# A spectral block's forward stage as a written plan of single steps, with all of xn on VectorE

## The chip, the cores and the metric

The kernel runs on one core of a Trainium2 chip. The metric is the time of one execution on the device in microseconds, the median of three runs. In the profile PE is TensorE's matmuls and PEld its weight loads, DVE is VectorE, ACT is ScalarE, POOL is GpSimd, SP is the engine that issues most DMAs.

## The reference, cut to what matters

```python
x = A_x                                                     # (1, 2048, 640) bf16
sa, ca, ga, sb, cb, gb = silu(c) @ w_mod, in six rows of 640
h = layernorm(x) * (1 + ca) + sa
x = x + ga * irfft2(rfft2(h) * (w_r + 1j * w_i))            # spectral mixing
h = layernorm(x) * (1 + cb) + sb
x = x + gb * ((silu(h @ w_gate) * (h @ w_up)) @ w_down)     # 1728 hidden columns
```

The two-dimensional Fourier transforms over 2048 x 640 are done as matmuls with tables of cosines and sines.

## The kernel before

The 2048 rows are 16 tiles of 128 rows (row = 16 p + t). Everything is emitted in the order in which it stands in the code: the schedule is manual, each engine executes its instructions in that order, and a tile framework adds the semaphore waits. A pool with `bufs=n` gives n buffers to one name; the next tile of that name waits until the oldest is free.

**Head** (lines 201 to 231 and 353 to 381). SP issues all early loads in one order: x tiles, `wm_ca`, the DFT table `Rp`, the tables `Gtab`, then the spectral weights (`Wneg`, `Wb`, `Wq`), `wm_sa`, `Ktab` and `wm_g`; none of them waits for compute. TensorE runs warm-up matmuls (`keep_warm`, `w_ps`), 44 and later 6. `mod_cols` (25 matmuls with one column) gives 1 + ca, and `Rs` is `Rp` scaled by it, four pieces on VectorE and two on ScalarE.

**Forward stage** (L277 to L426). For a tile t:

- statistics: two `bn_stats` halves and an aggregate on VectorE (`st`, `mv`; L280, L282)
- rstd: a square root on ScalarE (L251), a reciprocal on VectorE (L292); from tile 4 on for two tiles at once
- xn = (x - mean) * rstd (L297): on VectorE, and on GpSimd for tiles 7, 9, 11 and 13
- five transposes on TensorE into `t1ps` (L303), copied from PSUM to `hT`: by ScalarE (L306) for odd tiles and tile 0, by VectorE (L308) otherwise
- dfwd: six matmuls of 328 columns with `Rs` into `zps` (L319), copied to Z by ScalarE (L327), for tile 14 by VectorE
- s1: four matmuls of 328 columns with `Gtab` into `aps` (L331, L332; one buffer), copied by ScalarE into `A_sb` (L345)

Tile 15 goes in two halves (`zE`, `zO`, `apsh`). A loop over t interleaves square roots, transposes and statistics of later tiles with dfwd(t) and s1(t - 1). After t = 14 VectorE negates the spectral weights in two instructions (L425, L426). `mod_sa` (25 matmuls into `mpsB`, then `sa_col` on VectorE) ends the stage.

**Product stage** (L448 to L619). Columns are worked in 11 units, ten of them with four groups and one, the third, with a single group; the first three are transposed by TensorE (`t2`, copied to `B2`), the others by DMA transposes that SP issues when `A_sb` is full and Gtab's memory is free. A unit: `stage_a` (`xps`, copied to X by ScalarE; GpSimd then adds `shat` to one partition of X), `product` (PP, VectorE), `stage_b` (`yps`, L498; copied to Y2), `stage_c` (`eps_`, copied to Ep by ScalarE). `mod_shat` computes `shat` from `sa_col`: six matmuls into `sps`, E to SBUF on ScalarE, two `scalar_tensor_tensor` on VectorE. In the first round of the loop `m_ps` (50 matmuls) gives the gates' columns, which ScalarE copies out. After it come the inverse transforms (L677 to L722) and the feed-forward (L732 to the end).

The loop of the forward stage, in its core:

```python
for t in range(2, NT + 1):
    if t % 2 == 0 and t < NT - 2:
        ln1_sqrt(t + 2, t + 4)
    if 4 <= t < NT - 1:
        t1(t + 1)
...
    if 4 <= t < NT:
        dfwd(t)
    if t >= 4:
        s1(t - 1)
```

Of the kernel before, what the change touches and what calls it, by code (L numbers as in the profile page):

```python
# [18 lines left out]
LH = 164  # L19
# [116 lines left out]
def adaln_block_kernel(  # L136
# [46 lines left out]
    sE = const.tile([1, 2, LH], F32, name="sE")  # L183
# [87 lines left out]
    with tc.tile_pool(name="ph1", bufs=3) as ph1, \  # L271
# [5 lines left out]
        def ln1_half(t, h):  # L277
            if h == 0:
                sts[t] = ph1.tile([P, 2, 6], F32, name="st")
            nc.vector.bn_stats(sts[t][:, h, :], x_sb[:, t, 320 * h:320 * h + 320])  # L280
            if h == 1:
                nc.vector.bn_aggr(mv1[:, t, :], sts.pop(t)[:])  # L282

        def ln1_stats(t):
            ln1_half(t, 0)
            ln1_half(t, 1)
# [7 lines left out]
        def ln1_xn(t):  # L294
            xns[t] = ph1.tile([P, D], BF16, name="xn")
            eng = nc.gpsimd if t in (7, 9, 11, 13) else nc.vector
            eng.tensor_scalar(xns[t][:], x_sb[:, t, :], mv1[:, t, 0:1], rstd1[:, t:t + 1], ALU.subtract, ALU.mult)  # L297

        def t1(t):
            xn = xns.pop(t)  # L300
            t1ps = ps1.tile([P, NC5, 128], BF16, name="t1ps")
            for c5 in range(NC5):
                nc.tensor.transpose(t1ps[:, c5, :], block(xn, c5), identb[:])  # L303
            hTs[t] = ph1.tile([P, NC5, 128], BF16, name="hT")
            if t % 2 == 1 or t == 0:
                nc.scalar.copy(hTs[t][:], t1ps[:])  # L306
            else:
                nc.vector.tensor_copy(hTs[t][:], t1ps[:])  # L308

        def dfwd(t):  # L310
            hT = hTs.pop(t)
            if t == NT - 1:
                zs = [ps1.tile([P, 512], F32, name=n, tag="t1ps") for n in ("zE", "zO")]
            else:
                zps = ps1.tile([P, 2, 512], F32, name="zps")
                zs = [zps[:, 0], zps[:, 1]]
            for r in range(2):
                for i in range(3):
                    nc.tensor.matmul(zs[r][:, :L], lhsT=hT[:, 2 * r + i, :], rhs=Rs[:, 3 * r + i, :],  # L319
                                     start=(i == 0), stop=(i == 2))  # L320
            if t == NT - 1:
                Zs[t] = [ph1.tile([P, L], BF16, name=n, bufs=1) for n in ("ZE", "ZO")]
                nc.scalar.copy(Zs[t][0][:], zs[0][:, :L])
                nc.vector.tensor_copy(Zs[t][1][:], zs[1][:, :L])
            else:
                Zs[t] = ph1.tile([P, 2, 2, LH], BF16, name="Z")
                (nc.vector.tensor_copy if t == NT - 2 else nc.scalar.copy)(Zs[t][:].rearrange("p r c l -> p r (c l)"), zps[:, :, :L])  # L327
# [5 lines left out]

        def s1(t):
            Z = Zs.pop(t)
            if t == NT - 1:
                for r, eng in ((0, nc.scalar.copy), (1, nc.vector.tensor_copy)):
                    aps = ps1.tile([P, 2, 256], F32, name="apsh", tag="zps")
                    s1_into(t, [aps[:, c, :LH] for c in range(2)], Z[r][:, 0:LH], Z[r][:, LH:L])
                    eng(A_sb[:, NG * r:NG * r + NG, t].rearrange("p l c j -> p c l j"),  # L340
                        aps[:, :, :LH].rearrange("p c (l j) -> p c l j", j=4))
                return
            aps = ps1.tile([P, 2, 512], F32, name="aps", tag="aps", bufs=1)
            s1_into(t, [aps[:, c, :L] for c in range(2)], Z[:, :, 0, :], Z[:, :, 1, :])
            nc.scalar.copy(A_sb[:, :, t, :, :].rearrange("p l c j -> p c l j"),  # L345
                           aps[:, :, :L].rearrange("p c (l j) -> p c l j", j=4))

        def mod_sa():
            mpsB = ps1.tile([P, NC5], F32, name="mpsB", tag="t1ps")
            mod_cols(mpsB, wm_sa, 0, True)  # L350
            nc.vector.tensor_copy(sa_col[:], mpsB[:])
# [4 lines left out]
        keep_warm(ps1, "t1ps", 2, 44)  # L356
# [3 lines left out]
        ln1_stats(0)  # L360
        ln1_sqrt(0, 1)
        ln1_stats(1)
        ln1_sqrt(1, 2)
        ln1_recip(0, 1)
        ln1_xn(0)
        ln1_recip(1, 2)
        ln1_xn(1)
# [3 lines left out]
        t1(0)  # L371
# [6 lines left out]
        t1(1)  # L378
        keep_warm(ps1, "t1ps", 2, 6)
        ln1_stats(2)  # L380
        ln1_sqrt(2, 3)
        dfwd(0)
        dfwd(1)
        ln1_half(3, 0)
        ln1_recip(2, 3)
        ln1_xn(2)
        ln1_half(3, 1)
        ln1_sqrt(3, 4)
        t1(2)
        s1(0)  # L390
        ln1_half(4, 0)
        ln1_recip(3, 4)
        ln1_xn(3)
        ln1_half(4, 1)
        dfwd(2)
        t1(3)
        s1(1)
        ln1_stats(5)
        for t in range(2, NT + 1):
            if t % 2 == 0 and t < NT - 2:  # L400
                ln1_sqrt(t + 2, t + 4)
            if 4 <= t < NT - 1:
                t1(t + 1)
            if t == 3:
                dfwd(3)
                s1(2)
                t1(4)
            if t + 4 < NT:
                ln1_half(t + 4, 0)
            if t % 2 == 0 and t + 2 < NT:  # L410
                ln1_recip(t + 2, t + 4)
                if t + 3 in (7, 9, 11, 13):
                    ln1_xn(t + 3)
            if t + 2 < NT and t + 2 not in (7, 9, 11, 13):
                ln1_xn(t + 2)
            if t + 4 < NT:
                ln1_half(t + 4, 1)
            if 4 <= t < NT:
                dfwd(t)
            if t >= 4:  # L420
                s1(t - 1)
            if t == NT:
                mod_sa()
            if t == 14:
                nc.vector.tensor_scalar_mul(Wb[:, 0, :, 0:161], Wb[:, 2, :, 0:161], -1.0)  # L425
                nc.vector.tensor_scalar_mul(Wq[:, 2], Wq[:, 0], -1.0)  # L426
# [10 lines left out]
    with tc.tile_pool(name="ph2", bufs=2) as ph2, \  # L437
# [13 lines left out]
        def t2(u):  # L451
            n = len(units[u])
            for h in range(2):
                t2ps = ps2.tile([P, 4, 128], BF16, name="t2ps", bufs=2)
                for i, g in enumerate(units[u]):
                    nc.tensor.transpose(t2ps[:, i, :], A_sb[:, NG * h + g, :, :, :].rearrange("p t c j -> p (t c j)"), identb[:])
                B2 = ph2.tile([P, 4, 128], BF16, name="B2", bufs=4)
                if h == 0:
                    nc.scalar.copy(B2[:, :n, :], t2ps[:, :n, :])
                else:  # L460
                    nc.vector.tensor_copy(B2[:, :n, :], t2ps[:, :n, :])
                for i, g in enumerate(units[u]):
                    B2s[NG * h + g] = B2[:, i, :]
# [76 lines left out]
        def mod_shat(l0, l1):  # L540

            sps = ps2.tile([1, 2, 256], F32, name="sps", tag="eps_", bufs=2)
            n = 2 * (l1 - l0)
            for r in range(2):
                for i in range(3):
                    nc.tensor.matmul(sps[:, r, :n], lhsT=sa_col[:, 2 * r + i:2 * r + i + 1],
                                     rhs=Rp[:, 3 * r + i, :].rearrange("p (c l) -> p c l", c=2)[:, :, l0:l1],
                                     start=(i == 0), stop=(i == 2))
            E = sE[:, :, l0:l1]
            O = sps[:, 1, :n].rearrange("p (c l) -> p c l", c=2)  # L550
            nc.scalar.activation(E, sps[:, 0, :n].rearrange("p (c l) -> p c l", c=2), ACT.Copy, scale=float(S))
            for h in range(2):
                nc.vector.scalar_tensor_tensor(shat[:, h, :, l0:l1], O, float(S) if h == 0 else -float(S), E, ALU.mult, ALU.add)

        t2(0)
        mod_shat(128, LH)
        Xs[0] = stage_a(0)
        t2(1)
        for it in range(NU + 2):
            if it == 0:  # L560
                PPs[0] = [product(0, 0, Xs[0][0])]
# [4 lines left out]
            if it == 0:  # L566
                mod_shat(0, 128)
                m_ps = ps2.tile([P, 2, NC5], F32, name="m_ps", tag="eps_", bufs=2)
# [5 lines left out]
            if it < NU:  # L574
                X = Xs.pop(it)
                if it > 0:
                    PPs[it] = [product(it, 0, X[0])]
            if 0 <= it - 1 < NU:
                PP = PPs.pop(it - 1)
                Y2s[it - 1] = []  # L580
                for h in range(len(PP)):
                    yps = stage_b(it - 1, h, PP[h])
                    Y2s[it - 1].append(evict_y(it - 1, h, yps))
            if it < NU and len(X) > 1:
                PPs[it].append(product(it, 1, X[1]))
            if it == 1:
# [249 lines left out]
```

## Time and profile before

| | us |
|---|---|
| median of three runs (lowest, highest) | 284.66 (284.05, 284.86) |
| the profiled execution | 284.62 |
| its span | 282.40 |
| head, to the first matmul of dfwd(0) | 0 to 9.2 |
| forward stage, to the first matmul of `mpsB` | 9.2 to 41.3 |
| bridge, to the second unit's first `yps` | 41.3 to 51.2 |
| other units | to 77.4 |
| inverse transforms | 77.4 to 101.0 |
| feed-forward | 101.0 to 282.4 |

How to read it: times count from the start of the span. A row of a group gives line, engine, operation, output and inputs, then busy time, the mean of one in ns, and the idle time of the engine just before it with what ended it. A row of the waits gives the waiting engine, tile and line, then who released it: total, how often, the longest. The chain of waits is followed back from the last instruction to what released each step; it gives start, length and step. A wait for several things is put down to the last.

### The profile page before, as it was taken

To read this page: it belongs to the slowest core of one execution; us is meant where nothing else is said; L and a number is where in the kernel's file an instruction comes from. 1 tells how busy PE (TensorE), PEld (TensorE's weight loads), DVE (VectorE), ACT (ScalarE), POOL (GpSimd) and SP (SyncE) were. 2 spreads that over 40 slices of the span, in tenths; PEclk is the share of its full clock that TensorE was granted. 3 is DMA by queue.
4 is the path that set the end of the run, shared out by engine and by line. 5 is a ranking of instruction groups with operands and counts; after the bars stand their busy time and mean duration, and the time that the engine had idled before them with its cause. 6 is when DMAs were issued, how large, how long until landed. Compare 5 with 4: busy or idle time off the path is not lost.

```text
span 282.4 us, 5282 instructions
## 1 busy us (share of the span) xinstructions
PE 269.8 (96%) x2130; PEld 171.1 (61%) x2130; DVE 161.9 (57%) x408; ACT 114.0 (40%) x221; POOL 19.0 (7%) x34
## 2 busy tenths in 40 slices
PE   7979988999899999999999999999999999999995
PEld 7556667999687854445764445774444675444673
DVE  4897654799769847887225863323882422432322
ACT  5769875899555673223013224004223203223000
POOL 0026501322000010000000000000000000000000
PEclk9999999999999999999999999999999999999999
DMA  7979969999793401040110031011004011000011
GB/s 266 417 204 240 372 238 165 248 328 375 261 328 118 71 12 23 0 95 0 46 49 12 0 51 44 23 49 33 0 7 88 24 47 34 0 1 2 0 46 46
DMA packets 40634, 30.82 MB, mean 109 GB/s; under 512 B 29281, under 2 KB 37410, under 8 KB 40482
## 3 DMA queue, kind: packets, MB, share of 16 engines
q1 hardware_dynamic: 40608, 30.49, 36.9%
q8 instruction: 16, 0.26, 0.4%
q14 instruction: 8, 0.07, 0.1%
q10 hardware_dynamic: 2, 0.00, 0.0%
HBM read 22.88 MB, written 3.93 MB: 95 GB/s over the span
## 4 chain that ended last, share of the span: by engine, by line
PE 84%; DVE 7%; ACT 4%; POOL 2%; issue 1%; DMA 0%; ACTq 0%; POOLq 0%; DVEq 0%
PE gps L750 20%; PE ups L750 20%; PE ob L784 11%; PE oa L784 10%; PE yps L498 3%; PE zps L319 3%; POOL xn L297 2%; PE oa L699 2%; PE w_ps L267 2%; PE xps L473 2%; PE xps L474 2%; PE gu L737 2%; PE ob L699 1%; DVE x_sb L702 1%; PE t1ps L303 1%
## 5 line engine op out<-in xcount | busy, mean ns | idle before, releaser
L750 PE MATMUL gps<-h2T_all,Wg 128*128 128x512 bf16 x260 | 64.6, 379 | 0.0
L750 PE MATMUL ups<-h2T_all,Wu 128*128 128x512 bf16 x260 | 64.6, 379 | 0.0
L753 ACT ACTIVATE sg<-gps 128x512 f32<-128x512 f32 x52 | 31.1, 597 | 74.0 <-PE gps L750 72.3
L750 PEld LDWEIGHTS <-Wu 128*128 128x128 bf16 x260 | 25.4, 98 | 30.7
L750 PEld LDWEIGHTS <-Wg 128*128 128x128 bf16 x260 | 25.3, 98 | 30.5
L754 DVE TENSOR_TENSOR ATb<-ups,sg 128x512 bf16<-128x512 f32 x26 | 17.9, 690 | 32.0 <-PE ups L750 32.0
L754 DVE TENSOR_TENSOR ATa<-ups,sg 128x512 bf16<-128x512 f32 x26 | 17.9, 688 | 20.4 <-PE ups L750 17.5
L784 PEld LDWEIGHTS <-ATa 128*128 128x128 bf16 x224 | 21.9, 98 | 9.3 <-issue 0.5
L784 PEld LDWEIGHTS <-ATb 128*128 128x128 bf16 x224 | 21.9, 98 | 8.8
L740 ACT ACTIVATE sg<-gu 64x512 f32<-64x512 f32 x4 | 2.3, 587 | 46.6 <-PE gu L737 46.6
L786 DVE TENSOR_TENSOR xo<-ob,x_sb 128x320 bf16<-128x320 f32 x16 | 7.9, 491 | 22.1 <-PE ob L784 22.1
L786 DVE TENSOR_TENSOR xo<-oa,x_sb 128x320 bf16<-128x320 f32 x16 | 7.8, 490 | 18.4 <-PE oa L784 18.4
L784 PE MATMUL oa<-Wd_sb,ATa 128*128 128x320 bf16 x112 | 16.8, 299 | 0.1
L784 PE MATMUL oa<-Wd_sb,ATb 128*128 128x320 bf16 x112 | 16.5, 299 | 0.0
L784 PE MATMUL ob<-Wd_sb,ATb 128*128 128x320 bf16 x112 | 16.5, 299 | 0.0
L784 PE MATMUL ob<-Wd_sb,ATa 128*128 128x320 bf16 x112 | 16.5, 299 | 0.0
L319 PE MATMUL zps<-Rs,hT 128*128 128x328 bf16 x90 | 15.0, 303 | 0.6 <-ACT hT L306 0.4
L280 DVE BATCH_NORM_STATS2 st<-x_sb 128x6 f32<-128x320 bf16 x32 | 14.4, 472 | 0.8 <-DMA x_sb<-in_A_x_dram 0.8
L691 ACT CAST VT<-va 128x512 bf16<-128x512 f32 x16 | 9.4, 587 | 8.0 <-PE va L687 7.1
L498 PE MATMUL yps<-identb,PP 128*128 128x128 bf16 x162 | 11.7, 219 | 0.6 <-DVE PP L489 0.4
L297 POOL TENSOR_SCALAR xn<-x_sb,mv,rstd 128x640 bf16<-128x640 bf16 x4 | 10.6, 2656 | 21.3 <-PE zps L319 19.3
L476 ACT CAST X<-xps 128x512 bf16<-128x512 f32 (+1 forms) x21 | 11.3, 598 | 1.4 <-PE xps L474 1.4
(204 smaller groups left out, 415.4 us busy)
## 6 DMA issues: line engine op xcount, KB each, us to landing
out_dram<-xo SPq DMA_DIRECT2D x16, 160.0 KB, 1.8
Wg<-in_B_w_gate_dram SPq DMA_DIRECT2D x1, 2080.0 KB, 12.3
Wd_sb<-in_B_w_down_dram SPq DMA_DIRECT2D x1, 2080.0 KB, 13.1
Wu<-in_B_w_up_dram SPq DMA_DIRECT2D x1, 2080.0 KB, 8.4
x_sb<-in_A_x_dram SPq DMA_DIRECT2D x3, 640.0 KB, 9.2
wm_g<-in_w_mod_dram SPq DMA_DIRECT2D x2, 800.0 KB
Gtab<-tab_G SPq DMA_DIRECT2D x4, 384.0 KB, 7.8
Htab<-tab_H SPq DMA_DIRECT2D x1, 1536.0 KB, 7.7
```

Of the source, the lines that this page charges most:

```text
L280: nc.vector.bn_stats(sts[t][:, h, :], x_sb[:, t, 320 * h:320 * h + 320])
L297: eng.tensor_scalar(xns[t][:], x_sb[:, t, :], mv1[:, t, 0:1], rstd1[:, t:t + 1], ALU.subtract, ALU.mult)
L319: nc.tensor.matmul(zs[r][:, :L], lhsT=hT[:, 2 * r + i, :], rhs=Rs[:, 3 * r + i, :], start=(i == 0), stop=(i == 2))
L476: nc.scalar.copy(X[:, :n].rearrange("p i c k j -> p i (c k j)"), xps[:, :n, :])
L498: nc.tensor.matmul(yps[:, i, :], lhsT=PP[:, i, cp].rearrange("p a k j -> p (a k j)"), rhs=identb[:], start=(cp == 0), stop=(cp == 1))
L691: nc.scalar.copy(VTs[t][:, 0:4, :], va[:])
L699: nc.tensor.matmul(os_[odd][:], lhsT=VT[:, 2 * odd + ci if ci < 2 else 4, :], rhs=Rinv_sb[:, odd, ci, :], start=(ci == 0), stop=(ci == 2))
L750: nc.tensor.matmul(o[:], lhsT=w_[:, c5, fc * 128:(fc + 1) * 128], rhs=h2T[:, :, c5, :], start=(c5 == 0), stop=(c5 == NC5 - 1))
L753: nc.scalar.activation(sg[:], gps[:], ACT.Silu)
L754: nc.vector.tensor_tensor(AT[:, fc, :], ups[:], sg[:], ALU.mult)
L784: nc.tensor.matmul(os_[h][:], lhsT=AT[:, fc, tok], rhs=Wd_sb[:, fc, h * 320:(h + 1) * 320], start=(fc == 0), stop=(fc == NFC - 1))
L786: nc.vector.tensor_tensor(xo[:, h * 320:(h + 1) * 320], os_[h][:], x1[:, t, h * 320:(h + 1) * 320], ALU.add)
```

## The change

The forward stage's loop is replaced by a string of single steps that a small interpreter emits in that order. A step is a letter and a tile: `s` with `a` or `b` is one half of the statistics, `g` the aggregate, `q` the square root, `r` the reciprocal, `n` xn, `T` the transposes, `h` the copy to hT, `D` dfwd, `Z` its copy, `S` s1, `A` its copy, `W` a negation; `d`, `z`, `u`, `v` are second halves of tile 15. What one function emitted together (transposes and their copy, statistics and aggregate) can now stand apart, so each engine gets an order of its own.

- xn is always on VectorE. The copies hT of tiles 6, 8, 10, 11, 12, 14, 15, Z of 13 and 14, and A of 10 and 11 are on VectorE, all others on ScalarE (before: hT of even tiles from 2 on and Z of 14 on VectorE).
- xn, hT and Z have four buffers instead of three, the statistics six.
- Head: 32 warm-up matmuls instead of 44; xn(0) comes before the rest of tile 1's statistics; tile 0's transposes and hT come before `mpsA`; 8 warm-ups instead of 6 after tile 1's transposes.
- The negations are cut in four: two at the end of the plan, two after the first `t2`.
- `sa_col` is copied by ScalarE. In `mod_shat` ScalarE copies E and O together and GpSimd adds and subtracts them. The B2 copies of the one-group unit are both on ScalarE.
- Both products of unit 0 come at once; `m_ps` and its copies move from the first round of the loop to the second, behind `stage_b` of unit 0.

```diff
         def ln1_xn(t):
-            xns[t] = ph1.tile([P, D], BF16, name="xn")
-            eng = nc.gpsimd if t in (7, 9, 11, 13) else nc.vector
-            eng.tensor_scalar(xns[t][:], x_sb[:, t, :], mv1[:, t, 0:1], rstd1[:, t:t + 1], ALU.subtract, ALU.mult)
+            xns[t] = ph1.tile([P, D], BF16, name="xn", bufs=4)
+            nc.vector.tensor_scalar(xns[t][:], x_sb[:, t, :], mv1[:, t, 0:1], rstd1[:, t:t + 1], ALU.subtract, ALU.mult)
...
+        def negate(i):
+            k = 8 * (i % 2)
+            o, a = ((Wb[:, 0, k:k + 8, 0:161], Wb[:, 2, k:k + 8, 0:161]), (Wq[:, 2, k:k + 8], Wq[:, 0, k:k + 8]))[i // 2]
+            nc.vector.tensor_scalar_mul(o, a, -1.0)
...
-            nc.vector.tensor_copy(sa_col[:], mpsB[:])
+            nc.scalar.copy(sa_col[:], mpsB[:])
...
-        keep_warm(ps1, "t1ps", 2, 44)
+        keep_warm(ps1, "t1ps", 2, 32)
...
+        HT_DVE, Z_DVE, A_DVE = [6, 8, 10, 11, 12, 14, 15], [13, 14], [10, 11]
+        pairs = {0: 1, 1: 2, 2: 3, 3: 4, 4: 6, 6: 8, 8: 10, 10: 12, 12: 14, 14: 16}
+        plan = (
+            "s2a D0 h1 s2b s3a D1 Z0 s3b g2 g3 S0 q2 q3 r2 Z1 r3 n2 A0 n3 T2 s5a T3 h2 s5b S1 s4b h3 D2 g5 s4a A1 "
+            "s6a D3 Z2 g4 s7a q4 s6b S2 Z3 r4 n4 A2 n5 T4 g6 T5 s7b h4 S3 s9a h5 g7 D4 s10a q6 s9b A3 D5 r6 n7 Z4 "
+            "n6 T7 s8b Z5 T6 g9 S4 h6 h7 s8a D6 A4 s10b g8 g10 S5 q8 s11b Z6 r8 D7 n8 A5 n9 T8 s13b Z7 S6 h8 T9 "
+            "s11a A6 D8 s12a h9 g11 s14a S7 s12b q10 Z8 D9 r10 n11 A7 n10 T11 g12 Z9 s13a T10 S8 h10 h11 D10 A8 "
+            "g13 s14b q12 s15a S9 Z10 r12 D11 n12 A9 g14 n13 T12 s15b Z11 S10 h12 T13 g15 A10 q14 D12 h13 r14 n14 "
+            "S11 Z12 n15 T14 A11 T15 D13 h14 h15 S12 Z13 D14 A12 S13 Z14 d15 A13 D15 z15 S14 Z15 u15 W0 A14 S15 "
+            "v15 A15 W1"
+        )
...
+        go("s0a s0b g0 q0 s1a r0 n0 s1b g1 q1 r1 n1 T0 h0")
         mpsA = ps1.tile([P, NC5], F32, name="mpsA", tag="aps", bufs=1)
         mod_cols(mpsA, wm_ca, 0, True)
...
-        t1(1)
-        keep_warm(ps1, "t1ps", 2, 6)
...
-            if t == 14:
-                nc.vector.tensor_scalar_mul(Wb[:, 0, :, 0:161], Wb[:, 2, :, 0:161], -1.0)
-                nc.vector.tensor_scalar_mul(Wq[:, 2], Wq[:, 0], -1.0)
+        go("T1")
+        keep_warm(ps1, "t1ps", 2, 8)
+        go(plan)
+        mod_sa()
...
-                if h == 0:
+                if h == 0 or n == 1:
                     nc.scalar.copy(B2[:, :n, :], t2ps[:, :n, :])
...
-            nc.scalar.activation(E, sps[:, 0, :n].rearrange("p (c l) -> p c l", c=2), ACT.Copy, scale=float(S))
+            nc.scalar.activation(sEO[:, :, :, l0:l1], sps[:, :, :n].rearrange("p r (c l) -> p r c l", c=2), ACT.Copy, scale=float(S))
             for h in range(2):
-                nc.vector.scalar_tensor_tensor(shat[:, h, :, l0:l1], O, float(S) if h == 0 else -float(S), E, ALU.mult, ALU.add)
+                nc.gpsimd.tensor_tensor(shat[:, h, :, l0:l1], sEO[:, 0, :, l0:l1], sEO[:, 1, :, l0:l1],
+                                        ALU.add if h == 0 else ALU.subtract)
 
         t2(0)
+        negate(2)
+        negate(3)
         mod_shat(128, LH)
...
             if it == 0:
-                PPs[0] = [product(0, 0, Xs[0][0])]
+                PPs[0] = [product(0, h, X) for h, X in enumerate(Xs.pop(0))]
...
             if it == 0:
                 mod_shat(0, 128)
+            if 0 < it < NU:
+                X = Xs.pop(it)
+                PPs[it] = [product(it, 0, X[0])]
+            if 0 <= it - 1 < NU:
+                PP = PPs.pop(it - 1)
...
+            if 0 < it < NU and len(X) > 1:
+                PPs[it].append(product(it, 1, X[1]))
+            if it == 1:
                 m_ps = ps2.tile([P, 2, NC5], F32, name="m_ps", tag="eps_", bufs=2)
                 mod_cols(m_ps[:, 0], wm_g, 0)
                 mod_cols(m_ps[:, 1], wm_g, 1)
```

## The prediction

> **What bounds the kernel now.** The profiled execution took 284.62 us: a span of 282.40 and 2.22 around it; the median of the three runs is 284.66, so sums made on this execution are moved by +0.04. I read the page's first two parts, then the busy time by stretch.
>
> ```profile
> PE 269.8 (96%) x2130; PEld 171.1 (61%) x2130; DVE 161.9 (57%) x408; ACT 114.0 (40%) x221; POOL 19.0 (7%) x34
> POOL 0026501322000010000000000000000000000000
> ```
>
> ```profile
> core 0: us, PE busy (x) PEld busy (x) DVE busy (x) ACT busy (x) POOL busy (x), PEclk, DMA share, GB/s
> 21.90:33.30 11.40, 10.57 (x91) 7.25 (x92) 8.84 (x27) 9.96 (x19) 7.96 (x4) 1.00 1.09 291
> 33.30:41.30 8.00, 7.50 (x65) 5.28 (x66) 4.21 (x9) 6.87 (x13) 0.00 (x0) 1.00 0.83 311
> 41.30:51.10 9.80, 8.48 (x173) 7.29 (x171) 5.73 (x17) 5.21 (x17) 1.63 (x5) 1.00 0.92 152
> 51.10:77.40 26.30, 25.12 (x369) 23.17 (x367) 22.85 (x55) 22.23 (x44) 5.10 (x17) 1.00 0.97 313
> ```
>
> TensorE is "96% busy" over the span, but that is an average: from 101 us to the end the feed-forward is all TensorE, and the diff leaves it alone. What it edits lies before 51 us. There no engine is full, and GpSimd, little used elsewhere, is 70% busy in the middle of the forward stage. The chain of waits says why:
>
> ```profile
> 22.86 2.71 POOL xn L297
> 25.61 0.45 PE t1ps L303 x5
> 26.06 0.84 PE zps L319 x6
> ...
> 28.66 0.71 ACT Z L327
> 29.37 0.61 ACT A_sb L345
> 29.98 0.20 ACT rstd L251
> 30.20 0.18 DVE rstd L292
> ...
> 30.63 2.61 POOL xn L297
> ...
> 38.20 0.84 DVE Z L327
> 39.04 0.74 DVE Wb L425
> 39.78 0.73 DVE Wq L426
> 40.52 0.42 DVE ZO L324
> ```
>
> It is a ring over two tiles: the slow GpSimd xn, its transposes, matmuls, ScalarE's copies, the square root that had to queue behind them, the reciprocal, the next GpSimd xn. The transposes of tiles 7 and 13 start at 21.97 and 33.28, so the ring takes 3.77 us for two tiles. At the end of the stage VectorE puts two negations (1.47) between Z of tile 14 and the last copy that TensorE needs.
>
> **The forward stage after.** Two tiles cost TensorE 2 x (5 x 0.056 + 10 x 0.139) = 3.34 us by the spacing of its instructions in the timeline, so 0.43 of each ring is to be had. The price of moving xn:
>
> ```profile
> L297 POOL TENSOR_SCALAR xn<-x_sb,mv,rstd 128x640 bf16<-128x640 bf16 x4 | 10.6, 2656 | 21.3 <-PE zps L319 19.3 <-DVE rstd L292 1.0 <-PE t1ps L303 0.9
> L297 DVE TENSOR_SCALAR xn<-x_sb,mv,rstd 128x640 bf16<-128x640 bf16 x3 | 1.3, 447 | 0.1
> ```
>
> 2.66 us of GpSimd become 0.36 of VectorE four times over (447 ns, of which the last 0.085 overlap the next instruction, as all VectorE costs below are counted). The Trainium skill, "GPSIMD Engine Reference", Engine selection, says that a one-input elementwise operation on GpSimd runs at about line rate; Elementwise — side-by-side cycle accounting gives 1.03 cycles an element, an estimate of 0.55 us for this xn. By that there would be no ring to break and the move would only load VectorE. The trace has 2.66 beside 0.45, and the trace decides.
>
> VectorE now becomes the engine to sum. Head first: its x tile still lands at 3.80. In the new order xn(0) goes ahead of the second statistics half of tile 1: g0 4.72, square root 4.96 to 5.25, reciprocal 5.30, xn(0) 5.48, s1b 5.84, g1 6.35, square root to 6.89, reciprocal 6.93, xn(1) 7.11 to 7.46, one_p_ca, four Rs of 0.22 from 7.66. Statistics of tile 2 start at 8.5 instead of 8.87. On ScalarE hT(0) now runs before the two Rs instead of delaying them (they ended at 9.72, now about 8.7), so tile 1's matmuls come about 1.0 earlier; that is cover, not a second gain, since VectorE sets the pace from here.
>
> From 8.5 through Z of tile 14 the plan gives VectorE: 28 statistics halves at 0.43 = 12.0; 14 aggregates at 0.12 = 1.7, now apart from their halves; 8 reciprocals at 0.20, which includes the wait of the following xn, = 1.6; 14 xn = 5.0; 7 hT at 0.40 = 2.8; 2 Z at 0.76 = 1.5; 2 A copies = 1.5. Sum 26.2. An A copy on VectorE is not in the trace: I take Z's 842 ns, the same size from PSUM; bounds 0.71, what it takes on ScalarE, and 1.1 should the scattered write cost (the half-size pair, 498 scattered and 492 flat, says it does not). ScalarE falls to about 13 Z, 13 A, 9 hT at 0.61 and 8 roots at 0.2, some 23 us, and TensorE's 16 tiles make 26.7 from 8.4, with less to do at the end. Neither is ahead of VectorE. More buffers (four xn, hT and Z, six sets of statistics) cost nothing and are what lets the aggregates stand apart.
>
> To 26.2 comes VectorE's idle time. Its rows of before:
>
> ```profile
> DVE rstd L292 <- ACT rstd L251: 3.0, 6, 0.9
> ...
> PEld L303 <- POOL xn L297: 2.6, 4, 0.9
> ...
> DVE hT L308 <- PE t1ps L303: 1.2, 3, 0.5
> ```
>
> (The middle row is TensorE's, waiting for GpSimd; it goes with the move.) The low end is none, the high end VectorE's two rows, 4.2. Setting the plan's steps down one after another with the rows' durations, most reciprocals find their root done, because the plan puts a step or two between aggregate, root and reciprocal: about 1.1 is left. The same done for the old order reaches the end of the stage 0.4 too early, so I take 1.5. Z(14) then ends at 8.5 + 26.2 + 1.5 = 36.2; before, 39.04. The negations are gone from the tail (W0, 0.44, stands between ZO and the last A copy, beside TensorE's last matmuls; uncovered it costs 0.4). Before it was 2.2 from there to mpsB (41.26); now the matmuls of tiles 14 and 15 set it, about 1.85. mpsB at 38.05: **3.2 earlier**, between 4.7 and 0.5.
>
> Covers: the loads keep their times, since they are queued without waiting for compute. wm_sa must be there for mpsB: issued at 28.15 with 8.6 to landing, 36.8, so 1.3 to spare; if mpsB came before 36.8 the rest would be lost. Six DMA transposes on SP move up with the stage, behind wm_g, whose packets end at about 41; the first pair is needed nine microseconds after the stage, and landed within 6 of issue before.
>
> **The bridge to the product stage.** Count from mpsB's start M. Before, the second unit's yps began at 51.18, M + 9.92. After: sa_col on ScalarE (0.17, as on VectorE), t2 M + 1.04, first xps M + 2.16, second M + 4.5: unchanged. Then unit 0's second product no longer waits behind shat, so yps(0) comes at M + 6.75 and not 7.76. But the 50 matmuls of m_ps, 1.33, which ran in TensorE's wait for that product, now follow yps(0): M + 8.98; ga_col, gT M + 9.4; 16 xps, 0.9; yps(1) at M + 10.35. That loses 0.45. ScalarE gets sa_col, the second one-column B2 (0.28) and a longer sEO (+0.23) just where it starts to be the bound (five evictions at 0.53 = 2.66 a unit from here on); I let 0.25 through. **Loss 0.7**, between 0 and 1.5.
>
> shat on GpSimd is new: two adds of 256 elements on one partition, ahead of unit 2's X add in its queue, for which unit 2's product, and VectorE's queue behind it, waits. Bounds 0.24 (an add of 32 elements) and 2.66 (xn, 640); I take 1.06, xn's 4.15 ns an element. By the layout each may take 2.3 before yps(2) is late; at 2.66 it costs 0.7. The four quarter negations (0.44 each by half of the old 0.83) lie where VectorE waits for X: nothing, or 0.4 if the product is late.
>
> From yps(1) on units, tiles and feed-forward follow each other as before; the weights they need are issued from inside the same loop and move along. So 3.2 - 0.7 = 2.5: 284.62 - 2.5 + 0.04 = **282.2 us**.
>
> **Rivals.** *Half the gain or none.* VectorE, now the pace-maker, idles in its fixed order: every reciprocal waits for a root behind 0.71 us copies, every hT for transposes. Against: roots were late because they followed a GpSimd ring. With 2.9 of idle the gain is 1.1 (283.6); with before's 4.2 it is gone (284.9). *Slower: the TensorE clock.* The first 44 warm-up matmuls are 0.107 apart until 6.92, the transposes at 7.62 only 0.055: full rate came between, although the profile's granted clock says 1.00 throughout. After, 32 warm-ups end near 5.7, with gaps up to 8.4. If the rate stays halved, each tile costs TensorE 1.67 more; it has about 2.8 of slack in the stage, so with 2.5 of gain it decides from the fourth tile (1.67 x 4 = 6.7); with six it is 10.0 - 2.8 - 2.5 = +4.7, 289.4. Against: TensorE still works for most of 4 to 10 us. The skill's "TensorE: Matmul & The Clock Gate", Part 1, has a free-running window of 3.4 us that must be busy; by that one missed window costs about two tiles, inside the slack. *More gain*: half that idle and the 0.45 of m_ps hidden, 3.7, 281.0. *The move does nothing*, because something else in the ring is as long: against it stands TensorE's 3.34 beside 3.77, and POOL as the chain's named link.
>
> **How the numbers follow.** About 0.3%, 0.85 us, is what a measurement of this kernel can tell from no change. Forecast (281.2 to 283.0) 0.62; half the gain (283.0 to 283.8) 0.14; more 0.06; none, within 0.85, 0.09; slower, by the clock or a shat above 4.0 us (2.3 + 3.35 / 2), 0.09. Faster 0.82, same 0.09, slower 0.09. The range 281.1 to 283.7 takes the forecast and nearly all of its two neighbours.
>
> **What would show it.** Right: no POOL xn; VectorE nearly without gaps from 8.5 to 36; mpsB near 38; yps(1) near 48.7; the feed-forward's first matmul near 98.5 for 101.0. Wrong in the first step: reciprocals still behind L251 for 3 us. Wrong in the bridge: TensorE waiting for PP behind POOL shat. Clock: matmuls of D0 at 0.27 apart.

## The result, and the profile after

| | before | after |
|---|---|---|
| median, us (lowest to highest) | 284.62 (284.05 to 284.86), 4 runs | 280.63 (280.36 to 281.39), 4 runs |
| profiled execution; its span | 284.62; 282.4 | 280.83; 279.0 |

The ratio is 0.9867, with an interval from 0.9842 to 0.9892: 4.0 us faster. The prediction had the direction, but 282.2 us, and a range that began at 281.1. From the page's first two parts:

```profile
PE 268.6 (96%) x2120; PEld 170.3 (61%) x2120; DVE 163.6 (59%) x411; ACT 112.8 (40%) x220; POOL 10.5 (4%) x34
POOL 1000023312000010000000000000000000000000
```

GpSimd has lost its 10.6 us of xn. What it does now, from 39.9 on and behind a little set-up in the first slice, is shat and the adds to X. The busy time by stretch, for the stretches shown of before:

```profile
core 0: us, PE busy (x) PEld busy (x) DVE busy (x) ACT busy (x) POOL busy (x), PEclk, DMA share, GB/s
21.90:33.30 11.40, 11.37 (x106) 8.20 (x105) 10.94 (x33) 8.77 (x16) 0.00 (x0) 1.00 1.05 276
33.30:41.30 8.00, 7.08 (x94) 5.27 (x91) 4.75 (x10) 4.74 (x10) 1.16 (x3) 1.00 1.27 353
41.30:51.10 9.80, 8.83 (x157) 7.96 (x158) 6.44 (x17) 7.13 (x20) 3.16 (x10) 1.00 1.01 156
```

In the first row TensorE is busy 11.37 of 11.40 us (10.57 before), and VectorE 10.94 (8.84). The waits between 8.5 and 36 us, where before had 3.0 us of reciprocals behind L251:

```profile
ACT A_sb L343 <- PE aps L333: 3.0, 3, 1.8
PEld L301 <- DVE xn L293: 1.5, 3, 0.9
...
DVE Z L318 <- PE zps L309: 0.5, 1, 0.5
...
DVE rstd L289 <- ACT rstd L251: 0.2, 1, 0.2
```

VectorE waits for one root, 0.2, and once 0.5 for TensorE. The chain of waits leaves the engines at the end of the stage and runs through a load:

```profile
28.25 0.37 SPq L223
28.67 8.84 DMA wm_sa<-in_w_mod_dram
37.55 0.79 PE mpsB L243 x25
```

The stage's own last matmul starts at 36.94; mpsB then waits for wm_sa until 37.55. Read at five points of the trace (starts, us):

| kernel | dfwd(0) | dfwd(4) | last matmul of tile 15 | mpsB | yps(1) | from dfwd(4) to that last matmul |
|---|---|---|---|---|---|---|
| before | 9.18 | 18.23 | 41.19 | 41.26 | 51.18 | 22.96 |
| after | 8.42 | 16.70 | 36.94 | 37.55 | 47.77 | 20.24 |
| difference | -0.76 | -1.53 | -4.25 | -3.71 | -3.41 | -2.72 |

From there nothing changes: the feed-forward's first matmul came at 97.50 for 100.90, 3.40 earlier, and the span is 3.4 shorter. Another 0.39 lies around the span: 1.83 us for 2.22.

### The profile page after: what moved, and what is told of

It reads as the page before. It is cut to its first block, busy times and chain, and to the rows that moved or that the text cites. A ratio compares the mean times of both kernels' runs of the same rounds, so it can differ in the third digit from the quotient of the medians.

```text
span 279.0 us, 5262 instructions
## 1 busy us (share of the span) xinstructions
PE 268.6 (96%) x2120; PEld 170.3 (61%) x2120; DVE 163.6 (59%) x411; ACT 112.8 (40%) x220; POOL 10.5 (4%) x34
## 4 chain that ended last, share of the span: by engine, by line
PE 74%; DMA 10%; SPq 9%; DVE 4%; ACT 1%; issue 1%; ACTq 0%; DVEq 0%
PE gps L740 20%; PE ups L740 20%; PE ob L774 11%; PE oa L774 10%; DMA Wd_sb<-in_B_w_down_dram 4%; SPq L218 4%; DMA wm_sa<-in_w_mod_dram 3%; DMA Gtab<-tab_G 2%; PE oa L689 2%; SPq L596 2%; PE gu L727 2%; PE ob L689 1%; DVE x_sb L692 1%; SPq L223 1%; PE yps L488 1%; PE xps L463 1%
## 5 line engine op out<-in xcount | busy, mean ns | idle before, releaser
L740 PEld LDWEIGHTS <-Wu 128*128 128x128 bf16 x260 | 25.5, 98 | 30.6
L774 PEld LDWEIGHTS <-ATa 128*128 128x128 bf16 x224 | 21.9, 98 | 9.3 <-issue 0.5
L774 PEld LDWEIGHTS <-ATb 128*128 128x128 bf16 x224 | 21.9, 98 | 8.8
L280 DVE BATCH_NORM_STATS2 st<-x_sb 128x6 f32<-128x320 bf16 x32 | 13.8, 470 | 0.8 <-DMA x_sb<-in_A_x_dram 0.8
L309 PEld LDWEIGHTS <-hT 128*128 128x128 bf16 x96 | 8.8, 98 | 4.8 <-ACT hT L305 0.8
```

The lines of the kernel that those rows point to most:

```text
L309: nc.tensor.matmul(zap, lhsT=hTs[t][:, 2 * r + i, :], rhs=Rs[:, 3 * r + i, :], start=(i == 0), stop=(i == 2))
L740: nc.tensor.matmul(o[:], lhsT=w_[:, c5, fc * 128:(fc + 1) * 128], rhs=h2T[:, :, c5, :], start=(c5 == 0), stop=(c5 == NC5 - 1))
L774: nc.tensor.matmul(os_[h][:], lhsT=AT[:, fc, tok], rhs=Wd_sb[:, fc, h * 320:(h + 1) * 320], start=(fc == 0), stop=(fc == NFC - 1))
```

## The experiments

All are compared with the kernel before, run on the same chip beside them. The last column of the table above is kept as a measure, "dfwd(4) to the end", since it is free of what happens in the head; it is not free of work that an edit moves to the time before dfwd(4).

**1. xn on VectorE alone.**

```diff
# in the kernel before
-            eng = nc.gpsimd if t in (7, 9, 11, 13) else nc.vector
+            eng = nc.vector
```

> The kernel before with one line changed: xn of tiles 7, 9, 11 and 13 is on VectorE too; order, buffers, head and product stage stay. Theory A (the prediction's: the GpSimd xn is what holds the stage, 3.77 us for two tiles beside TensorE's 3.34): most of the measured 4.0 comes from this line alone, some 2 to 3, so about 282 us. Theory B (the order written out per engine is what pays; in the old order VectorE would now do xn of two tiles in a row ahead of what ScalarE and TensorE wait for): nothing or a loss; setting the old order's steps down with the durations of the rows puts mpsB 0.9 later than before, 42.1, so about 285.5 us.

284.42 us, ratio 0.9993 (0.9979 to 1.0006): no change. The spans grew, 282.6 in the middle for 282.4, and what lies around them shrank, 1.82 for 2.16. mpsB came at 41.21 (41.26 before), and dfwd(4) to the end took 23.28 us (22.96). (The profiled execution is the longest of the ten, 285.11: its clock dropped from 43.8 to 47.2, behind what is read here.) There is still a ring, without GpSimd. The chain of waits of this run, one round of two tiles:

```profile
20.96 0.70 ACT Z L327
21.66 0.61 ACT A_sb L345
22.27 0.20 ACT rstd L251
...
22.50 0.18 DVE rstd L292
...
22.70 0.81 DVE xn L297 x2
...
23.56 0.45 PE t1ps L303 x5
24.01 0.85 PE zps L319 x6
...
24.94 0.70 ACT Z L327
```

From Z to Z 3.98 us. The root stands on ScalarE behind Z and A, which wait for matmuls that wait for the xn before. It is not the ring of before. There, one turn goes from the xn of tile 9 (22.86) to that of tile 13 (30.63), 7.77 us for four tiles, and TensorE waits for GpSimd ahead of tiles 7, 9, 11 and 13; here it waits for VectorE ahead of tiles 8, 10 and 12. The transposes of tile 7 in before and of tile 8 in this run:

```profile
21.97 0.45 PE L303 MATMUL t1ps<-identb,xn 128*128 128x128 bf16 x5 [0.51 <-POOL xn L297]
```

```profile
23.56 0.45 PE L303 MATMUL t1ps<-identb,xn 128*128 128x128 bf16 x5 [0.46 <-DVE xn L297]
```

So GpSimd's xn was a link of the old ring, but a second ring, as long for its two tiles, stood right behind it. Part of that is the old order too: it emits the xn of tile 9 ahead of that of tile 8, and both (0.81) lie in the ring. The two in the other order were not tried. Theory A, the prediction's, falls.

**2. The plan, with the four xn back on GpSimd.** The same line, in the kernel after, with GpSimd for tiles 7, 9, 11 and 13.

> The kernel after with one line changed: xn of tiles 7, 9, 11 and 13 is on GpSimd again, in the plan's order. Theory A (the ring of GpSimd is what held the stage before): about the time before, 284 to 285 us, mpsB near 41. Theory B (order and engine only pay together: the plan leaves little room between reciprocal, xn and transposes, so each 2.66 us xn is waited for in full): clearly above the time before; setting the plan's steps down with 2.66 for these four gives mpsB at 43.7, 6 us later than after, so about 286.5 us.

287.43 us, ratio 1.0107 (1.0079 to 1.0135): slower than before, as theory B had it and by a little more (mpsB at 44.13, dfwd(4) to the end 27.28). The four slow xn cost the stage 7.0 us beside after's 20.24. Part of that is the clock: in the profiled execution TensorE waited 2.0 us for the first of them, to 20.60, and from 21.5 to 23.7 its matmuls of 328 columns were 0.27 us apart instead of 0.14; the granted clock was 0.92 between 15.3 and 21.9 and 0.90 between 21.9 and 33.3. Over the whole span it was 0.994 in this execution (287.77) and 0.988 in another (288.61), but 1.00 in the other two, and these took 287.01 and 287.10. So with or without it the plan is slower with these xn on GpSimd than the old order was. A plan written for a slow xn was not tried.

**3. The root's place, in the old order.** The kernel of experiment 1, with statistics one tile further ahead and roots one round earlier:

```diff
-            if t % 2 == 0 and t < NT - 2:
-                ln1_sqrt(t + 2, t + 4)
+            if t == 2:
+                ln1_sqrt(4, 6)
+            if t % 2 == 1 and t + 1 < NT - 2:
+                ln1_sqrt(t + 3, t + 5)
...
-            if t + 4 < NT:
-                ln1_half(t + 4, 0)      # and ln1_half(t + 4, 1) likewise
+            if t == 2:
+                ln1_stats(6)
+            if t + 5 < NT:
+                ln1_half(t + 5, 0)
```

> The kernel of the first run (the kernel before with all xn on VectorE) with one more change of order: statistics run one tile further ahead, and each pair's square root stands one round earlier in ScalarE's queue, ahead of two Z and two A copies. In the first run the stage kept a period of 3.98 us for two tiles, and VectorE waited 0.54 each time for a root that stood behind Z and A. Theory B (what held the stage is a ring closed by the order, the root behind the copies, whichever engine does xn): the waits of reciprocals go, the period falls to about 3.5, where ScalarE's own work for two tiles (two Z and two A at 0.61, one hT at 0.59, one root at 0.2: 3.2 to 3.5) holds it; mpsB about 1.0 before the first run's 41.2, near 40.2; about 283.5 us. Rival (the root's place is nothing, and the plan gains by its copies, its head and its tail): mpsB stays at 41 and the time at 284.4.

283.25 us, ratio 0.9948 (0.9933 to 0.9963); mpsB 40.39; dfwd(4) to the end 21.47, which is 1.81 less than in experiment 1. Of that, 0.57 only moved: the statistics of tile 6 now stand ahead of dfwd(4), which comes 9.65 us after dfwd(0) for 9.08 there. From dfwd(0) to the last matmul it is 31.12 for 32.36, so the roots' place is worth 1.24, about what the time shows. VectorE's wait for roots between 14 and 34 us fell from 1.9 to 0.4, and the chain now goes along TensorE:

```profile
22.30 0.28 PE t1ps L303 x5
22.58 0.84 PE zps L319 x6
...
23.97 0.28 PE t1ps L303 x5
24.25 0.83 PE zps L319 x6
25.09 0.23 PE aps L331
...
25.73 0.28 PE t1ps L303 x5
26.01 0.83 PE zps L319 x6
```

1.67 to 1.76 us a tile, 3.43 for two, about TensorE's 3.34. Early roots with xn still on GpSimd were not tried, so whether the old order needed the move at all stays open.

**4. The root's place, in the plan.** The plan with its roots behind the copies (on the denser head of experiment 6):

```diff
-S5 q8 s11b Z6 r8 D7 n8 A5 n9
+S5 s11b Z6 D7 A5 q8 r8 n8 n9       # the same for q6, q10, q12, q14
```

> The kernel with the denser head, and in the plan the square roots of the pairs 6 to 15 put back behind the copies Z and A (for the pair 10 and 11, for instance, the steps 'q8 s11b Z6 r8 D7 n8 A5 n9' become 's11b Z6 D7 A5 q8 r8 n8 n9'); xn stays on VectorE, split, buffers and all other steps as they are. Theory B (the gain comes from taking the root out of the ring of copies): the reciprocals wait for roots again and each pair's transposes wait for its xn; setting the steps down, mpsB comes 5.3 later, 42.3, later than before the change; about 285.6 us. Rival (the gain comes from the aggregate of plan, split and buffers, and the root's place is one small part of it): under 1.5 later, 281.7 us.

285.93 us, ratio 1.0048 (1.0033 to 1.0063); mpsB at 42.56, 5.6 later than with the roots in place (36.97 in experiment 6); dfwd(4) to the end 25.64. The waits between 8.5 and 41 us:

```profile
PEld L301 <- DVE xn L293: 7.2, 7, 1.5
ACT A_sb L343 <- PE aps L333: 6.7, 5, 3.0
DVE rstd L289 <- ACT rstd L251: 5.9, 6, 1.4
```

With all of xn on VectorE and everything else of the plan in place, five roots further back (with the reciprocals and xn that must follow them) undo more than the whole gain. Both directions agree: with xn on VectorE, the ring is closed by the root's place behind the copies on ScalarE.

**5. What sets the stage now.** Half the statistics left out, or computed twice, for tiles 6 to 11:

```diff
-            nc.vector.bn_stats(sts[t][:, h, :], x_sb[:, t, 320 * h:320 * h + 320])
+            if h == 0 or not 6 <= t < 12:
+                nc.vector.bn_stats(sts[t][:, h, :], x_sb[:, t, 320 * h:320 * h + 320])
```

> The kernel after with the second half of the statistics left out for tiles 6 to 11 (mean and variance come from the first 320 columns only): 6 x 0.43 = 2.6 us less on VectorE in the middle of the stage. Theory D (the prediction's: VectorE's sum sets the stage): the last matmuls of the stage (36.94 in after) come up to 2.6 earlier, at least 1. Theory E (after the change no single engine holds the stage: TensorE's 11.37 of 11.40 us between 21.9 and 33.3 and ScalarE's copies are level with VectorE): 0.0 to 0.3 earlier, 280.4 us.

> The kernel after with the second statistics half of tiles 6 to 11 computed twice: 6 x 0.43 = 2.6 us more on VectorE. Theory D (VectorE sets the stage) and theory E (all three level) both give about the full price: last matmuls of the stage near 39.6, 2.6 later, 283.2 us; setting the plan's steps down gives 2.9. Rival (VectorE has room in the plan, TensorE alone is the bound): under 1.0 later, 281.3 us.

The first took 281.53 us (ratio 0.9893, 0.9866 to 0.9921), 0.9 *more* than after; the second 282.71 (0.9939, 0.9915 to 0.9963). In both, as in the run with the old split of copies below, dfwd(0) started late, at 9.0, which experiment 6 explains. Freed of that, dfwd(4) to the end is 20.24 us with six halves less on VectorE, exactly after's, and 22.24 with six more (the second read on the slowest of its five executions, 283.96; the others took 282.64 to 282.87). Six halves are 2.4 us at the 0.40 for which each holds VectorE in the plan; the expectations reckoned with 0.43. VectorE is loaded to the brim but does not set the end. The less-statistics run on a denser head, where the clock is out of the way:

> The kernel with the denser head, with the second statistics half of tiles 6 to 11 left out (mean and variance from the first 320 columns only): VectorE has 2.6 us less, and the clock is not in the way. Theory D (VectorE's sum sets the stage, as the prediction had it): the last matmuls of the stage at 36.0 or earlier, 0.9 to 2.6 before after's 36.9. Theory E (TensorE sets it from about 15 us on): 36.7 to 36.9, under 0.2 earlier; 280.3 us.

280.41 us (0.9849, 0.9834 to 0.9864); last matmul at 36.96, for 36.90 of that head alone, 20.24 after dfwd(4). Theory D is refuted. The busy time by stretch of this run:

```profile
core 0: us, PE busy (x) PEld busy (x) DVE busy (x) ACT busy (x) POOL busy (x), PEclk, DMA share, GB/s
15.30:21.90 6.60, 6.45 (x56) 4.42 (x57) 4.62 (x18) 6.55 (x13) 0.00 (x0) 1.00 0.81 175
21.90:33.30 11.40, 11.37 (x106) 8.21 (x105) 10.79 (x32) 8.79 (x16) 0.00 (x0) 1.00 1.07 276
33.30:37.00 3.70, 3.70 (x31) 2.58 (x29) 2.49 (x5) 2.19 (x4) 0.00 (x0) 1.00 1.06 379
```

TensorE is all but full in the three; VectorE has 2.0 us free in the first. ScalarE is as full as TensorE in the first, 6.55 of 6.60, and no run relieves it alone. Less work on TensorE instead:

```diff
+            k = 2 if 6 <= t < 12 else 3       # on the denser head
-            for i in range(3):
+            for i in range(k):
```

> The kernel with the denser head, with one of three matmuls left out in each half of dfwd for tiles 6 to 11 (a part of the transform's sum is missing): 12 x 0.139 = 1.67 us less on TensorE. Theory G (TensorE alone sets the stage from 15 us on): the last matmuls of the stage 1.2 to 1.7 earlier than 36.9, near 35.4. Theory E in full (the three engines are level, so taking from any one gains little): under 0.3 earlier; setting the steps down gives 0.06. mpsB itself then waits for wm_sa, which lands near 37 or a little later, so the time is 280.2 us in both.

280.18 us (0.9840, 0.9824 to 0.9857); 19.84 from dfwd(4) to the last matmul: 0.40 of the 1.67 taken away. TensorE sets the stage, but with 0.4 us to the next limit; "level" (under 0.3) is a little too strong. The next limit is VectorE, on which the chain of waits of this run lies from 19.3 to 25.2:

```profile
19.31 0.49 DVE hT L305
19.80 0.79 DVE st L280 x2
...
24.77 0.46 DVE xn L293
```

The 2.4 us put on VectorE above, which cost 2.0, give it the same 0.4 of room. And the copies shared as before (`HT_DVE` the even tiles from 2, `Z_DVE` 14, `A_DVE` none):

> The kernel after with the copies shared as before: hT of the even tiles from 2 and Z of 14 on VectorE, no A there; the plan's order stays. ScalarE gets A of 10 and 11, Z of 13 and two hT more, less two early hT: some 2 us in the second half. Theory E (three engines level, so the split counts): the last matmuls of the stage about 1.0 later, 38.0, setting the steps down 1.06 at mpsB: about 281.6 us. Rival (only the order counts, ScalarE has room): under 0.3, 280.8 us.

281.57 us (0.9886, 0.9862 to 0.9911), with the late head; dfwd(4) to the end 20.70. The new split is worth 0.46, under half of the 1.0 that I expected.

**The filling, 8.6 to 15 us.** On the denser head, half the statistics of tiles 2 to 5 left out:

> The kernel with the denser head, with the second statistics half left out for tiles 2 to 5 (their mean and variance come from the first 320 columns): 4 x 0.43 = 1.7 us less on VectorE before 15 us. Between 8.6 and 15 us the chain of waits of after runs through statistics, xn and ScalarE's copies, and TensorE waits for xn there. Theory H (VectorE sets the filling of the stage, TensorE what comes after): the transposes of tile 4 (15.36 with the denser head) come 0.5 to 1.7 earlier and all up to the last matmuls of the stage (36.9) with them; setting the steps down gives 0.46 at the end. Rival (the filling is set by x, which lands as it lands, or by ScalarE): under 0.2 earlier.

280.78 us (0.9863, 0.9844 to 0.9881). dfwd(4) came at 16.46 for 16.66: 0.2, where theory H had 0.5 to 1.7. In this run's chain of waits ScalarE holds the filling with Z, two roots, Z, A, hT, hT, A, Z from 9.55 to 14.2. That is a reading and not shown: in the run with the old split, hT of tiles 2 and 4 is off ScalarE, and dfwd(4) came 8.99 after dfwd(0), as in the first run with half the statistics (9.02), which had the late clock too. What sets the filling stays open. That the time did not even fall by 0.2 is wm_sa: SP issued it only at 30.05 and mpsB started at 37.79, 1.1 after the last matmul's start.

**6. The head and the TensorE clock.** The timeline of PE in after, and in the first run with half the statistics:

```profile
6.03 0.45 PE L301 MATMUL t1ps<-identb,xn 128*128 128x128 bf16 x5
7.97 0.61 PE L267 MATMUL w_ps<-identb 128*128 128x128 bf16 x8
8.42 1.98 PE L309 MATMUL zps<-Rs,hT 128*128 128x328 bf16 x12
```

```profile
5.98 0.71 PE L302 MATMUL t1ps<-identb,xn 128*128 128x128 bf16 x5
8.14 1.06 PE L267 MATMUL w_ps<-identb 128*128 128x128 bf16 x8
8.99 3.04 PE L310 MATMUL zps<-Rs,hT 128*128 128x328 bf16 x12
```

The same twelve matmuls take 1.98 us and 3.04: 0.14 to 0.15 apart in the one, but for a wait between the two tiles, and 0.273 for the first nine of the other. The column of the granted clock reads 1.00 in both for these times, but the trace's record of the clock begins only at 5.91 in the one and at 11.44 in the other, which is where the rate doubles. Of the seven profiles with after's head four had the early rate and three the late one.

```diff
-        keep_warm(ps1, "t1ps", 2, 32)
+        keep_warm(ps1, "t1ps", 2, 36)
...
         mod_cols(mpsA, wm_ca, 0, True)
+        keep_warm(ps1, "t1ps", 2, 5)
```

> The kernel after with 36 warm-up matmuls instead of 32 and five more behind mpsA, so that TensorE works without a gap from 2.4 us to dfwd(0); nothing else. Why: in the profiles of the last three runs the matmuls of dfwd(0) and dfwd(1) were 0.273 to 0.274 apart and the stage began at 9.0, in the after profile and four others 0.139 to 0.150 apart from 8.3 to 8.4 on; the after kernel's own four times spread over 1.0 us (280.36 to 281.39). Theory F (after's shorter, broken warm-up sometimes misses the point at which the clock is raised, in a part of the executions, whatever else the kernel does): here all executions lie within 0.5 us of one another, dfwd(0)'s matmuls are 0.14 apart, median 280.4. Rival (the half rate came with the edits of those runs or at random, whatever the head): the spread of 1 us stays, median 280.8.

280.25 us, ratio 0.9843 (0.9828 to 0.9857), its four runs between 280.23 and 280.29. In all seven profiles with this head the rate had doubled before dfwd(0). Theory F holds. With fewer instead, 12 for 32:

> The kernel after with 12 warm-up matmuls instead of 32, so that TensorE idles from 3.7 to 6.0. Theory F: the clock is raised late in every execution, dfwd(0) and dfwd(1) at 0.27 a matmul, the last matmuls of the stage 1.3 later than after's 36.94, as in the run with half the statistics (38.25): about 281.7 us, all executions alike. The prediction's rival of the clock gave 289.4 if six tiles were at half rate: then the matmuls of dfwd(2) to dfwd(5) would be at 0.27 too. Rival (the clock rises from the load of the stage itself, whatever the warm-ups): 280.6 us.

281.81 us (0.9902, 0.9885 to 0.9918). dfwd(0) at 9.10, with 0.273 between its first matmuls and 0.14 from 10.7 on; dfwd(4) at 17.79, 1.13 later than with the denser head, and 20.24 from there, as always. So a late clock moves the whole stage by 1.1, a bit less than the 1.3 expected.

**7. The load.** `wm_sa` issued ahead of the two `Wq`:

> The kernel after with the load of wm_sa (0.8 MB) issued ahead of the two loads Wq and not behind them; nothing else. In the trace of after mpsB's weights wait 0.6 us and its matmuls 0.4 for that load, which lands near 37.5, while the last matmuls of the stage end near 37.0. Theory C (the load is the last to arrive, and cost 0.4 to 0.5): mpsB at 37.05 to 37.15, and all that follows 0.4 to 0.5 earlier: about 280.2 us. Rival (Wq, now one transfer later, near 35.6, or Ktab comes late for the negations, or mpsB has something else right behind the load): less than 0.2, 280.5 us.

281.11 us (0.9883, 0.9863 to 0.9903), from 280.18 to 281.50. The profiled execution did what theory C said: mpsB 36.94 right behind the last matmul (36.86), time 280.18. The median did not show it, because this kernel has after's head; its other times, 280.82 to 281.50, are of the size of the late ones above, though only the first was profiled. The load is no fixed cost: without the edit SP issued it between 27.8 and 30.05 us in the profiles, and mpsB lost 0.5 us to it in after, 1.0 in the run with fewer early statistics, and hardly anything in experiment 8.

**8. The bridge.** `m_ps` and its copies back in the loop's first round, behind the second `mod_shat`:

> The kernel after with the 50 matmuls of m_ps and their three copies back in the first round of the loop, behind the second mod_shat, where they stood before; nothing else. In after they run 45.07 to 46.31, between yps(0) and yps(1). The prediction's bridge: hidden in TensorE's wait for unit 0's second product, they would no longer delay yps(1), which then comes at mpsB plus 8.9 to 9.5 instead of plus 10.22: 0.7 to 1.3 earlier, setting the steps down 0.9, so about 279.7 us. Rival (ScalarE, with five evictions of 0.53 a unit, or VectorE's products set yps(1), and the three extra copies stand ahead of X): under 0.3, about 280.5 us.

279.83 us, ratio 0.9835 (0.9820 to 0.9849). mpsB 37.06, yps(1) 46.76: mpsB plus 9.70 instead of 10.22. The chain of waits:

```profile
43.41 1.33 PE m_ps L243 x50
44.88 0.89 PE yps L488 x16
46.92 0.89 PE yps L488 x16
```

m_ps stands in TensorE's wait ahead of yps(0), which comes 0.54 later than in after, but yps(1) follows it by 2.0 us instead of 3.6. That is 0.52, a little under the 0.7 to 1.3 expected; the other 0.49 by which yps(1) is ahead of after's 47.77 is the wait for wm_sa, which hardly occurred here.

**9. The price of the tail.** All four negations between Z(14) and ZO, on the denser head:

> The kernel with the denser head, with all four quarter negations on VectorE between Z of tile 14 and ZO, about where the two whole ones stood before. The prediction's tail: before, 2.2 us passed from the end of Z(14) to mpsB and it forecast 1.85 after; 1.5 us of negations in VectorE's queue ahead of ZO and the last A copy now delay mpsB by 0.5 to 1.3; setting the steps down 0.74: 281.0 us. Rival (TensorE's own matmuls cover them): under 0.2, 280.3 us.

281.34 us (0.9888, 0.9873 to 0.9903); dfwd(4) to the end 21.16, so 0.92, inside the 0.5 to 1.3 expected.

**10. The parts together.** Denser head, wm_sa first, m_ps in the first round:

> The kernel after with three edits together: the denser head (36 and five more warm-ups), the load of wm_sa ahead of Wq, and m_ps in the loop's first round. If the three are independent: mpsB at 37.0, yps(1) at 46.7, the span 278.0 or a little below, 279.7 us, and no execution over 280.1. If one undoes another (the wm_sa load moves Ktab or wm_g, which m_ps now needs 1.3 us sooner): yps(1) waits for a load, 280.3 us or more.

279.73 us, ratio 0.9824 (0.9810 to 0.9839), four runs between 279.70 and 279.76; span 278.0, mpsB 37.00, yps(1) 46.69. It beats both kernels, 5.0 under the 284.69 of before beside it, and no execution fell out of line.

## Why the prediction was wrong, step by step

**The mechanism** is the step that failed first. The prediction put ScalarE's copies and the root into its ring, then wrote that "roots were late because they followed a GpSimd ring" and priced the move. Experiment 1 shows them late, and the stage as long, without GpSimd. The ring had also been misread: one turn spans four tiles (7.77 us, 3.88 for two), and behind it stood one over two tiles that takes 3.98 when VectorE does xn. Both pass through a root behind Z and A on ScalarE, and with xn on VectorE it is that place which costs (experiments 3 and 4). From dfwd(0) to the last matmul before took 32.01, the move alone 32.36, with the roots' earlier place in the old order 31.12, and the whole plan 28.52. Of the last 2.60, 1.37 lie ahead of dfwd(4), which no run takes apart; the other 1.23 are about what the negations (0.92, experiment 9) and the split of copies (0.46, experiment 5) cost by themselves. To that comes the head, 0.76. "The move does nothing", because something else in the ring is as long, was given as a rival, but for the whole change; it is true of the move by itself.

**The sum** went by VectorE: start 8.5, work 26.2, idle 1.5, Z(14) done at 36.2. Measured: 8.60 and 35.30. In these 26.7 us VectorE is busy for 25.2, and its gaps add up to 1.5. With the waits of xn behind reciprocals (0.3) counted as work, as the prediction did, that is work 25.5 and idle 1.2. So the work was 0.7 too much: its largest term, 28 statistics halves at 0.43, took 0.40 each. The idle term was 0.3 too much; I had raised it from 1.1 to 1.5 since the same reckoning of the old order came out 0.4 early, and that correction did not carry over to another order. That VectorE sets the end was wrong: with six halves less the end stays (experiment 5). TensorE sets it, from 15 us on, with VectorE 0.4 behind. Its 26.7 from 8.4, which the prediction gave and set aside, end at 35.1, and what it waits, most of it in the filling (8.28 us from dfwd(0) to dfwd(4) for 6.68 of work by the spacing), brings them to 37.0; that VectorE's sum came out near is luck, in that the plan loads both almost alike.

**The tail** of 1.85 took 1.73, from 35.30 to about 37.03. **wm_sa**, estimated to land at 36.8 with what comes earlier lost, held mpsB to 37.55: the warning was right, the landing 0.7 later. Together mpsB came 0.5 ahead of the 38.05 forecast.

**The bridge** was to lose 0.7 and lost 0.30. m_ps behind yps(0) costs 0.52 (experiment 8), near the forecast (0.45). The other edits gained 0.22, where I had let 0.25 of ScalarE's work through; shat on GpSimd was far below the 1.06 that I took:

```profile
L541 POOL TENSOR_TENSOR shat<-sEO x4: 406/647/719, 39.9 to 45.3; 1x72 f32<-1x72 f32 x2, 1x256 f32<-1x256 f32 x2
```

Scaling by xn's 4.15 ns an element was too high by about half: the slowest of 256 elements took 0.72.

**Around the span** I carried 2.22 over; it was 1.83. Experiment 1 has the same 0.3 to 0.4 less from the move alone.

On the profiled execution these give 0.50 + 0.40 + 0.39 = 1.29 of the error; the remaining 0.3 is that execution against the median, 0.2, and rounding. The range had room for one of them: its low end stopped at the case "more gain", to which I gave 0.06, though the idle term's own bound was 0, and three small terms could err together on one side.

**The clock rival** happened in part. Three of seven profiles had dfwd(0) and most or all of dfwd(1) at 0.27. It was not six tiles but about two, and not "inside the slack": 1.1 us at the end of the stage, since TensorE had no such slack in this plan (busy 20.24 of the 20.30 us from dfwd(4) on). (By the prediction's own 1.67 a tile, a window of 3.4 us holds one tile at half rate, not two.) After's median of 280.63 lies 0.4 above the same plan with a denser head.

## What to carry to other kernels

When a chain of waits turns in a ring, count the tiles that one turn spans, and then look for the next ring, which the chain does not show: here four tiles with GpSimd's xn took 7.77 us, and two tiles with VectorE's took 3.98, so the faster engine bought nothing. What both have in common, here a root behind two copies in one queue, is the place to change. An order written by hand and the engine assignment it was written for are one change: each alone was worth nothing or cost 3 us here, together they gained 4. And once a stage is shortened, look at what was just in time before: a load that is issued late, a warm-up whose length nobody had to think about.

## What was not expected of the hardware

**The clock rises in steps, and missing one costs the stage 1.1 us.** The trace's record of the granted clock begins where the rate doubles. With the denser head that was at 4.93, 5.64, 6.66, 7.12, 7.24, 7.74 and 8.12 us, always before dfwd(0). With after's head, in which TensorE pauses for some 0.3 to 0.5 us near 5.8 and 7.3, it was at 5.23, 5.91, 6.69 and 7.13 in four profiles and at 11.25, 11.44 and 12.10 in three. Once up, the clock stays for a multiple of 3.41 us (13.65, 37.55 and 273.07 are 4, 11 and 80 times it), and the two drops in these traces, in experiments 1 and 2, lasted 3.41 each; the three late starts less one such step would have been 7.84 to 8.69. The Trainium skill, "TensorE: Matmul & The Clock Gate", Part 1, has a free-running window of 3.4 us of activity, and so a start that varies from run to run; the steps and the 3.2 us of spread with the denser head agree with that, and the spread is wider than the 500 ns either way that the same part gives for it. How short a pause may be was not tried, nor whether the pauses or the fewer matmuls decide.

**GpSimd's xn costs time outside the span.** With spans on record to 0.1, the time less the span was 2.11 to 2.25 us in the runs of before, 2.00 to 2.07 in experiment 2, and 1.73 to 1.86 in every other kernel, that of experiment 1 among them, which differs from before only in where four xn run. What is done in that time no trace here shows.
